# Attention and routed experts on one core: the last eight pairs of attention slots taken slot by slot

## The chip, the cores and the metric

One Trainium2 chip, one of its cores. The metric is the device time of one launch in microseconds; three runs of the kernel before gave a median of 679.24 us (677.79 to 680.12).

## The reference

```python
# q, k, v: (8, 8, 576, 64), s: (8, 8, 576); w_gate (512, 8), w_local (512, 1), w1 (8, 512, 1024), w2 (8, 1024, 512)
scores = scale * q @ k.T                              # per batch and head
cum = cumsum(maximum(s, 0))
bias = -(cum[:, None] - cum[None, :])                 # a weight of each key, falling with distance
scores = where(causal, -1e9, scores + minimum(bias, 0))
x = (exp(scores - max) / sum) @ v                     # to (batch, token, 8 heads * 64 = 512)
for b in range(8):
    for t in range(576):
        fresh = argmax(x[b, t] @ w_gate)
        e = fresh if t == 0 or sigmoid(x[b, t] @ w_local) < 0.5 else previous e
        out[b, t] = softmax(x[b, t] @ w_gate)[e] * (maximum(x[b, t] @ w1[e], 0) @ w2[e])
```

All in float32. A token's expert depends on the token before it, so the routing is a scan along each batch.

## The kernel before

The order of every instruction is written by hand: the code's order is each engine's order, and waits come from the data, from buffers that have to come free, and from events on which a transfer or a scatter is hung by `held`.

*The attention* (the first 203 us) runs over 32 slots `n`, one for a batch and two of its heads. Keys are cut in blocks of 128 and the triangle of the causal mask is skipped. A slot has

- `scores(n, u)`, u = 0, 1, 2: products of keys and queries into two PSUM banks (tile `ps`), exponential on ScalarE into tile `e`, masks of the diagonal on GpSimd (`masked`);
- `scores_halves`: the same for the 64x64 blocks that stand half over the diagonal (`ph`, `eh`, lines 1236 and 1238). `HALVES` names four of them per slot, which lie on the upper and the lower 64 partitions; a fifth, the last block (index `NH - 1`), lies on 64 partitions as well;
- `values_halves(n)` and `values(n, part)`: products of those weights with the values `vg` (lines 1288 and 1275), summed in a room of two PSUM banks, one bank for each part of the slot. Before the change the last block's products are the last steps of `values`, as 128-row products whose other 64 rows meet zeros;
- `evacuate(n, part)`: VectorE reads the sums, a reciprocal and a product for each part, into the token rows `xb`;
- `turn(n)`: a 32x32 transpose for the router; `weigh(n)`: values times key weights for a later slot (`WEIGHED` says up to which slot, after which pair).

Products in float32 take two passes, so each appears in the profile as two rows of PE and two weight loads (PEld).

Slots go in pairs `m`: scores of both slots, then the sums of both. The first slot's room is `po0`, `po1`, two banks of their own (`ps_o`); the second slot's is `pb`, taken from the ring of three two-bank buffers (`ps_s`) that also serves `ps`, `ph`, `lp` and `pos`.

*The router* works on groups of two batches, eight slots. `plan(m, place, f)` puts a piece of it into pair m: 0 and 1 behind the scores of the first and the second slot, 3 and 4 behind their sums, 5 at the pair's end. `product` (`lp`, TensorE), `logits`, `codes`, `turn1`, `turn2` (a scan on VectorE), `ranks` (`pos`, TensorE), `rows` and `gates` make each token's row in a table in DRAM; `scatter` stores 128 such rows by an indirect DMA from GpSimd, 18 times per group (`STORES` has the places). `assign_early` counts the first blocks of the experts at place 1 of pair 11.

*The loads* of later q, k and v go through SP's queue in the order of `transfers`, each hung on an exponential or a reciprocal. *The experts* (from 203 us on) work through units of tokens with weights that stream from DRAM.

The heart of the old loop over pairs:

```python
po = room(a)
values_halves(a, po, m)
halves = banks("ph") if b + 1 < NPAIR else None
to = room(b)
scores_halves(m + 1, halves)
values_halves(b, to, True)
```

## Time and profile before

| | us |
|---|---|
| median of three runs | 679.24 |
| the profiled execution | 680.58 |
| its span | 678.8 |
| attention, up to the first product of the experts | 202.57 |
| TensorE busy in the span | 662.1 |
| VectorE, GpSimd, ScalarE busy | 492.5, 369.6, 195.3 |

The profile is of one execution. "PE" are TensorE's products, "PEld" its weight loads; "issue" is idle time with no releaser in the profile. In the chain of waits a row has its start, its length, its engine, tile and line. DMA queue q8 carries instructions.

### The profile page before, as it was taken

How to read it: one execution, taken by the hardware profiler on the slowest of the kernel's cores; microseconds unless marked ns; L12 is line 12 of the kernel's file. 1: busy time of each engine (PE TensorE's matmuls, PEld its weight loads, DVE VectorE, ACT ScalarE, POOL GpSimd, SP SyncE). 2: the span in 40 equal slices, each digit the busy share in tenths (PEclk: the TensorE clock that was granted, in tenths of full speed). 3: DMA queues.
4: the chain of work that ended last, by engine and by line, in shares of the span. 5: the costliest groups of instructions: out<-in, count | busy, mean ns of one | idle time of the engine just before them, and what ended most of it. 6: DMA issues, size and time to landing. Idle time of an engine off the chain costs nothing.

```text
span 678.8 us, 18449 instructions
## 1 busy us (share of the span) xinstructions
PE 662.1 (98%) x7501; PEld 571.4 (84%) x7501; DVE 492.5 (73%) x942; ACT 195.3 (29%) x353; POOL 369.6 (54%) x525
## 2 busy tenths in 40 slices
PE   8999999999999999999999999999999999999995
PEld 7888877877788899999999999999589687796884
DVE  4665856886867799878988988955467664766843
ACT  4555635535522212212122122212211111111111
POOL 3562476776744888964555557540642542714733
PEclk9999999999999999999999999999999999999998
DMA  8665665766659798579977565616949796943002
GB/s 263 193 183 158 197 219 151 215 214 210 197 133 392 240 327 288 191 255 364 344 274 231 204 187 186 241 55 235 354 66 386 271 361 132 295 148 112 28 14 76
DMA packets 56549, 145.75 MB, mean 215 GB/s; under 512 B 13104, under 2 KB 33968, under 8 KB 51464
## 3 DMA queue, kind: packets, MB, share of 16 engines
q1 hardware_dynamic: 47352, 124.23, 55.8%
q0 software_dynamic: 9008, 20.11, 8.2%
q8 instruction: 61, 1.00, 0.6%
q14 instruction: 32, 0.26, 0.1%
q10 hardware_dynamic: 96, 0.15, 0.1%
HBM read 123.83 MB, written 20.85 MB: 213 GB/s over the span
## 4 chain that ended last, share of the span: by engine, by line
PE 86%; DVE 6%; issue 4%; POOL 2%; ACT 0%; POOLq 0%; DVEq 0%
PE p L731 26%; PE p L738 25%; PE ps L1218 11%; PE po L1275 6%; PE pb L1275 6%; PE hp L865 3%; PE yp L888 2%; PE hp L856 2%; PE lp L238 1%; PE ph L1236 1%; POOL out_dram L840 1%; DVE wt L655 1%; PE po L1288 1%; DVE w2b L655 1%; PE warm L1142 1%
## 5 line engine op out<-in xcount | busy, mean ns | idle before, releaser
L738 PE MATMUL p<-w2b,hT 128*128 128x256 f32 (+1 forms) x720 | 163.0, 379 | 0.0
L738 PEld LDWEIGHTS p<-w2b,hT 128*128 128x128 f32 (+1 forms) x720 | 133.3, 187 | 21.9 <-PE hp L856 1.6
L731 PE MATMUL p<-xTs,w1b 128*128 128x128 f32 (+1 forms) x1040 | 142.9, 295 | 0.0
L731 PEld LDWEIGHTS p<-xTs,w1b 128*128 128x128 f32 x1040 | 137.9, 191 | 3.6 <-issue 1.6
L1219 ACT ACTIVATE e<-ps 128x768 f32<-128x768 f32 (+1 forms) x96 | 76.4, 885 | 64.1 <-PE ps L1218 58.1
L840 POOL DMA_INDIRECT out_dram<-y,gi x37 | 46.9, 1269 | 74.2 <-ACT y L767 66.3
L767 ACT ACTIVATE y<-y,gi 128x256 f32<-128x256 f32 (+1 forms) x71 | 34.5, 505 | 161.6 <-DVE y L763 161.6
L771 ACT ACTIVATE hT<-hT 128x512 f32<-128x512 f32 (+1 forms) x52 | 36.8, 711 | 143.7 <-DVE hT L763 143.7
L1218 PE MATMUL ps<-qb,kb 64*128 64x384 f32 (+4 forms) x516 | 77.5, 446 | 0.2 <-ACT e L1219 0.2
L1218 PEld LDWEIGHTS ps<-qb,kb 64*128 64x128 f32 x516 | 47.7, 189 | 27.5 <-ACT e L1219 10.3
L371 POOL DMA_INDIRECT table<-xb,idx x54 | 57.3, 1062 | 15.8 <-issue 14.4
L738 PE MATMUL p<-wt,hSs 128*128 128x256 f32 (+1 forms) x272 | 63.3, 379 | 0.0
L710 POOL TENSOR_TENSOR hT<-hT,hSs 128x512 f32<-128x512 f32 (+1 forms) x14 | 21.1, 1508 | 76.8 <-PE p L738 76.8
L731 PE MATMUL p<-xSs,wt 128*128 128x128 f32 (+1 forms) x416 | 58.9, 295 | 0.5 <-DVE wt L655 0.5
L738 PEld LDWEIGHTS p<-wt,hSs 128*128 128x128 f32 (+1 forms) x272 | 50.7, 186 | 8.0
L1202 POOL TENSOR_SCALAR_AFFINE_SELECT e<-e 128x128 f32<-128x128 f32 (+1 forms) x96 | 35.7, 394 | 38.5 <-ACT e L1219 38.2
L731 PEld LDWEIGHTS p<-xSs,wt 128*128 128x128 f32 x416 | 55.6, 192 | 1.2 <-PE p L731 0.7
L763 DVE TENSOR_TENSOR hT<-p,sa 128x512 f32<-128x512 f32 (+1 forms) x48 | 31.2, 666 | 32.7 <-PE p L731 32.7
L1275 PE MATMUL pb<-vg,e 128*64 128x66 f32 x1280 | 41.9, 223 | 4.7 <-issue 4.7
L1275 PEld LDWEIGHTS pb<-vg,e 128*64 128x64 f32 x1280 | 39.7, 138 | 5.6 <-issue 5.4
L1275 PE MATMUL po<-vg,e 128*64 128x66 f32 x1280 | 41.6, 223 | 1.6 <-issue 1.6
L1275 PEld LDWEIGHTS po<-vg,e 128*64 128x64 f32 x1280 | 39.0, 138 | 3.2 <-issue 2.1
(304 smaller groups left out, 951.9 us busy)
## 6 DMA issues: line engine op xcount, KB each, us to landing
w2b<-in_w_dram SPq DMA_DIRECT2D x20, 2048.0 KB, 13.5
w1b<-in_w_dram SPq DMA_DIRECT2D x19, 2048.0 KB, 10.5
va<-in_v_dram SPq DMA_DIRECT2D x32, 320.0 KB, 3.4
xq<-table SPq DMA_DIRECT2D x72, 130.0 KB, 3.7
kb<-in_k_dram SPq DMA_DIRECT2D x31, 288.0 KB, 4.2
qb<-in_q_dram SPq DMA_DIRECT2D x31, 288.0 KB, 3.3
w1b<-in_w_dram SPq DMA_DIRECT2D x4, 512.0 KB
table<-xb,idx POOLq DMA_INDIRECT x54, 5.1
```

The source lines that it names most:

```text
L371: put = self.nc.gpsimd.indirect_dma_start(out=self.halves, in_=src, element_offset=0, in_offset=None, out_offset=bass.IndirectOffsetOnAxis ...
L710: self.adder(u, layer).tensor_tensor(a12, a12, (self.xS, self.hS)[layer][u][1], op=Alu.subtract)
L731: mm(ps[:, m * h : m * h + h], lhsT=b[:, k, (c * of + m) * P : (c * of + m) * P + P], rhs=a[:, k, :], start=m == 0 and k == 0, stop=m == o ...
L738: mm(ps[:p, c * w : c * w + w], lhsT=a[:, k, c * p : c * p + p], rhs=b[:, k, :], start=c == 0 and k == 0, stop=c == parts - 1 and k == n - 1)
L763: nc.vector.tensor_tensor(to[:, c], part, s[:, c], op=Alu.add)
L767: ins = nc.scalar.mul(to[:, c], to[:, c], gi[:p, parts * r + c, 1:2]).ins
L771: return gated(to, r) if layer else nc.scalar.activation(to, to, Act.Relu).ins
L840: put = nc.gpsimd.indirect_dma_start(out=out, out_offset=bass.IndirectOffsetOnAxis(ap=idx, axis=0), in_=y, element_offset=0, bounds_check= ...
L1202: nc.gpsimd.affine_select(out=ap, in_=ap, compare_op=Alu.is_ge, fill=0.0, base=base, pattern=n, channel_multiplier=-1)
L1218: mm(ps[:, h, at : at + z - a], lhsT=kb[d, key : key + P], rhs=qb[d, a:z], start=True, stop=True)
L1219: exps[n, u] = nc.scalar.activation(e[:, :, : WIDTH[u]], ps, Act.Exp, scale=scale).ins
L1275: of = mm(po[part][d, j - a, :], lhsT=weights_of(n, c, j, h), rhs=vgs[n % NV][:, c if j < 2 * G1 else G1 + c, h, :], start=(first and i == ...
```

## The change

- Pairs 8 to 15 are taken in halves. For n above 16: scores of slot n, the halves' scores of slot n + 1, then opening the room, halves and sums of slot n - 1, its reads and `after(n - 1)`. The values of a pair so stand behind the scores of the next slots. Slots of these pairs all use `po0`, `po1`, except the last one. The first eight pairs keep the old order.
- The last block's products move from `values` into `values_halves`, always on the lower 64 partitions. `eh` is per slot; its exponential is two instructions per slot (64 x 4 columns on 128 partitions, 128 columns on 64) and its masks are two (64x256 and 64x384).
- In pairs 8 and later `ranks`, `rows` and `gates` stand behind the first slot's sums (place 3) and not behind the second slot's scores.
- `codes` moves to a new place 2, behind the first slot's turn; the end of `turn2` becomes `turn3`, two places later; `weigh` is spread over slots; scatters are held by the end of the value products and no longer by a copy of the reciprocal; `STORES` changes.

TensorE, from slot 27's scores on before (pair 13), and from slot 26's on now (`ps` scores, `ph` halves' scores, line 1288 or 1298 the halves' products, line 1275 or 1285 the other products of values):

```order
L1218 MATMUL ps<-qb,kb 128x512 x2
L1218 MATMUL ps<-qb,kb 128x384 x2
L1218 MATMUL ps<-qb,kb 128x256 x2
L1218 MATMUL ps<-qb,kb 128x128 x2
L1288 MATMUL po_3302<-vg_137,eh 64x66 x2
L1288 MATMUL po_3303<-vg_137,eh 64x66 x2
L1288 MATMUL po_3302<-vg_137,eh 64x66 x2
L1288 MATMUL po_3303<-vg_137,eh 64x66 x2
L1236 MATMUL ph<-qb,kb 64x64 x20
L1288 MATMUL pb<-vg_138,eh 64x66 x8
L1275 MATMUL po_3302<-vg_137,e_3240 64x66 x6
```
```order
L1219 MATMUL ps<-qb,kb 128x512 x2
L1219 MATMUL ps<-qb,kb 128x384 x2
L1219 MATMUL ps<-qb,kb 128x256 x2
L1219 MATMUL ps<-qb,kb 128x128 x2
L1240 MATMUL ph<-qb,kb 64x64 x10
L1298 MATMUL po_3281<-vg_136,eh 64x66 x2
L1298 MATMUL po_3282<-vg_136,eh 64x66 x2
L1298 MATMUL po_3281<-vg_136,eh 64x66 x2
L1298 MATMUL po_3282<-vg_136,eh 64x66 x4
L1285 MATMUL po_3281<-vg_136,e_3073 64x66 x6
L1285 MATMUL po_3281<-vg_136,e_3074 64x66 x2
L1285 MATMUL po_3282<-vg_136,e_3073 64x66 x2
```

Between the scores stand the products of one slot instead of two, ph is split into ten and ten, and the last block's products (x4) stand with the halves.

VectorE, from slot 21's reads to the start of the early counting (`recs`, `xb` are the reads of the sums, `vg` a weighing, `xt` a turn, `cnt` the counting's first row):

```order
L1298 RECIPROCAL recs<-pb 128x8
L1298 TENSOR_TENSOR xb<-pb,recs 128x8x32
L1298 RECIPROCAL recs<-pb 128x10
L1298 TENSOR_TENSOR xb<-pb,recs 128x10x32
L1195 TENSOR_TENSOR vg_137<-va,wk 128x4x64
L1195 TENSOR_TENSOR vg_137<-va,wk 128x10x64
L1195 TENSOR_TENSOR vg_138<-va,wk 128x4x64
L1195 TENSOR_TENSOR vg_138<-va,wk 128x10x64
L1312 STREAM_TRANSPOSE xt_2719<-xb 128x9x2x32 x2
L388 TENSOR_TENSOR cnt<-base,base_631 128x8
```
```order
L1307 RECIPROCAL recs<-po_2755 128x8
L1307 TENSOR_TENSOR xb<-po_2755,recs 128x8x32
L1307 RECIPROCAL recs<-po_2756 128x10
L1307 TENSOR_TENSOR xb<-po_2756,recs 128x10x32
L1321 STREAM_TRANSPOSE xt_2713<-xb 128x9x2x32
L1196 TENSOR_TENSOR vg_138<-va,wk 128x4x64
L1196 TENSOR_TENSOR vg_138<-va,wk 128x10x64
L1196 TENSOR_TENSOR vg_135<-va,wk 128x4x64
L1196 TENSOR_TENSOR vg_135<-va,wk 128x10x64
L389 TENSOR_TENSOR cnt<-base,base_644 128x8
```

The two turns of a pair became one turn of a slot. Fourteen more rows of counting follow in both, and then the reads of slot 22: before, they free the room of slot 24, now that of slot 23.

GpSimd, masks and scatters (`e`, `eh` masks; `gap` and `table` one scatter) from the masks of slots 24 and 25 on before, and from those of slot 24 on now:

```order
L1202 AFFINE_SELECT e_2971<-e_2971 128x2x64
L1202 AFFINE_SELECT e_2972<-e_2972 128x2x64
L1202 AFFINE_SELECT e_2973<-e_2973 64x4x64
L1202 AFFINE_SELECT e_2995<-e_2995 128x2x64
L1202 AFFINE_SELECT e_2996<-e_2996 128x2x64
L1202 AFFINE_SELECT e_2997<-e_2997 64x4x64
L1202 AFFINE_SELECT eh<-eh 64x640
L1202 AFFINE_SELECT eh<-eh 128x640
L370 COPY gap<-recs 1x1
L371 DMA table<-xb,idx 75264x260
```
```order
L1203 AFFINE_SELECT e_2960<-e_2960 128x2x64
L1203 AFFINE_SELECT e_2961<-e_2961 128x2x64
L1203 AFFINE_SELECT e_2962<-e_2962 64x4x64
L1203 AFFINE_SELECT eh<-eh 64x256
L1203 AFFINE_SELECT eh<-eh 64x384
L371 MEMSET gap 1x1
L372 DMA table<-xb_1267,idx 75264x260
```

Six masks for a pair and two for its halves become three and two for a slot; three scatters follow each slot's masks there.

The diff, cut:

```diff
-NH = 2 * len(HALVES) + 1
+NH = len(HALVES) + 1
-WEIGHED = (3, 5, 9, 11, 11, 13, ...)
+WEIGHED = (1, 2, *(n + 2 - (n in (13, 21, 29)) for n in range(2, NPAIR)))
-STORES = (((3, 4, 5, 5, 5), ...
+STORES = (((3, 4, 5, 5, 5), (3, 4, 5, 5, 5), (3, 5, 5, 5), (3, 5, 5, 5)), ((5, 5, 5), (3, 3, 3, 5, 5, 5), (3, 3, 3, 5, 5, 5), (3, 3, 3)), ((5, 5, 5), (3, 3)))
+HALF_FROM = 8
...
         v.transpose(et, self.ei)
+        v.tensor_scalar(st["s1"], st["s1"], et[:, 31:32], None, Alu.max)
+
+    def turn3(self, g):
...
-    p_eh = pool("p_eh", 2)
+    p_eh = pool("p_eh", 3)
...
+        for j, n in enumerate(ns):
+            own = heads[1]
+            e = eh[n] = p_eh.tile([P, NH, 2, DH], F32, name="eh")
+            ps = ph[:, :, j * NH * DH : (j + 1) * NH * DH].rearrange("p h (n i) -> p n h i", i=DH)
+            for i, side, x in [*((t, side, x) for t, blocks in enumerate(HALVES) for side, x in zip(heads, blocks)), (NH - 1, own, NJ - 1)]:
...
+            nc.scalar.activation(e[:, : NH - 1], ps[:, : NH - 1], Act.Exp, scale=scale)
+            nc.scalar.activation(e[own, NH - 1], ps[own, NH - 1], Act.Exp, scale=scale)
+            for side in heads:
+                k = NH if side == own else NH - 1
+                masked(e[side, :k].rearrange("p n h i -> p (n h) i"), [[0, 2 * k], [1, DH]])
...
+    def apart_of(n):
+        return n % 2 and (n < 2 * HALF_FROM or n == NPAIR - 1)
     def room(n):
-        if n % 2:
+        if apart_of(n):
             po = banks("pb")
...
-        steps = [(j, c) for j in range(a, z) for c in [*range((j + 1) // 2), *([NF] if j == NJ - 1 else [])]]
+        steps = [(j, c) for j in range(a, z) for c in range((j + 1) // 2)]
...
     def values_halves(n, po, first):
+        todo.append((NH - 1, 1, side, NJ - 1, G1 + NF))
...
-        plan(m, 5, lambda g=g: (router.codes(g), router.turn1(g)))
+        plan(m, 2, lambda g=g: router.codes(g))
+        plan(m, 5, lambda g=g: router.turn1(g))
-        plan(m + 1, 1, lambda g=g: router.turn2(g))
+        plan(m + 1, 2, lambda g=g: router.turn2(g))
+        plan(m + 1, 5, lambda g=g: router.turn3(g))
+        p = 1 if m + 2 < HALF_FROM else 3
+        plan(m + 2, p, lambda g=g: router.ranks(g, banks))
...
-            after = {3: (2 * i, NJA), 4: (2 * i + 1, 0)}.get(p)
-            plan(i, p, lambda g=g, c=c, after=after, pair=pair: router.scatter(g, c, after, summed.get(pair)))
+            pair = {3: (2 * i, 1), 4: (2 * i + 1, 0), 5: (2 * i + 1, 1)}[p] if first else None
+            plan(i, p, lambda g=g, c=c, pair=pair: router.scatter(g, c, summed.get(pair)))
...
+        elif m < HALF_FROM:
+            of = {("e0", c): v_part(n), ("e2", c): v_part(n + 1), ("e1", c + 1): k0, ("v0", c): q0, ("v1", c): k1, ("v0", c + 1): q1}
+        else:
+            k = ("v0", c - 1) if m > HALF_FROM else ("e0", c + 1)
+            of = {("e0", c): v_part(n), ("e2", c): v_part(n + 1), k: k0, ("e1", c + 1): q0, ("e2", c + 1): k1, ("v0", c): q1} if n < NPAIR else {}
...
+    def after(n):
+        m, second = divmod(n, 2)
+        turn(n)
+        if second:
+            at(m, 5)
+        for i in range(WEIGHED[n] + 1, ...):
+            weigh(i)
+        if not second:
+            at(m, 2)
...
+        if m < HALF_FROM:
+            if second:
+                po = opened(n - 1)
+                scores_halves(n + 1, n + 2)
+                to = opened(n)
+                sums(n - 1, po)
+                sums(n, to)
+                after(n - 1)
+                after(n)
+        elif n > 2 * HALF_FROM:
+            scores_halves(n + 1)
+            sums(n - 1, opened(n - 1))
+            after(n - 1)
+    sums(NPAIR - 1, opened(NPAIR - 1))
+    after(NPAIR - 1)
```

`opened(n)` takes a room and runs `values_halves` in it; `sums(n, po)` runs `values` and `evacuate` for both parts and what is planned behind them.

## The prediction

> **What bounds the kernel now.** I read the page first, then what TensorE waits for, then the chain of waits in the attention (the first 203 us), then busy time by stretch and the DMA queues.

> ```profile
> span 678.8 us, 18449 instructions
> PE 662.1 (98%) x7501; PEld 571.4 (84%) x7501; DVE 492.5 (73%) x942; ACT 195.3 (29%) x353; POOL 369.6 (54%) x525
> ```

> TensorE is busy for 662.1 of 678.8 us, so the time is TensorE's work plus the moments in which it stands. The waits of PE in the attention are almost only these:

> ```profile
> PE pb L1275 <- issue: 4.7, 5, 1.4
> PE po L1275 <- issue: 1.6, 3, 1.1
> ```

> "issue" means that no semaphore explains the wait: eight pauses, 6.3 us, all inside the runs of value products. The chain shows where one sits (start, length, work):

> ```profile
> 41.67 4.67 PE ps L1218 x32
> 52.60 4.67 PE ps L1218 x32
> 155.99 2.31 PE lp L238 x64
> ```
> ```profile
> 165.90 4.67 PE ps L1218 x32
> 170.57 0.39 PE po L1288 x16
> 170.96 0.58 PE ph L1236 x40
> 171.54 0.23 PE pb L1288 x16
> 171.78 2.60 PE po L1275 x84
> 174.38 1.10 PE pb L1275 x37
> 175.48 1.40 issue
> 176.88 1.62 PE pb L1275 x47
> 178.50 4.67 PE ps L1218 x32
> ```

> An undisturbed pair of slots takes 52.60 - 41.67 = 10.93 us: 4.67 of scores (32 rows) and 6.26 of a burst (16+40+16+84+84 = 240 rows). The pair at 165.90 takes 12.60, which is 1.67 more for a named pause of 1.40. What the pauses are is seen when TensorE's rows are counted from the end of one to the end of the next (columns: stretch, us, PE, PEld, DVE, ACT, POOL, clock, DMA share, GB/s):

> ```profile
> 98.74:114.86 16.12, 15.03 (x383) 12.52 (x383) 9.21 (x19) 7.82 (x17) 10.63 (x19) 1.00 0.58 176
> 114.86:136.97 22.11, 21.80 (x508) 17.66 (x508) 19.20 (x58) 11.42 (x19) 14.80 (x32) 1.00 0.62 190
> 136.97:148.88 11.91, 10.62 (x254) 8.59 (x254) 10.73 (x32) 5.76 (x10) 9.30 (x19) 1.00 0.68 213
> 148.88:161.07 12.19, 11.12 (x254) 8.75 (x254) 8.13 (x16) 7.15 (x17) 8.78 (x15) 1.00 0.77 251
> 161.07:176.88 15.81, 14.41 (x383) 12.37 (x382) 12.08 (x41) 6.62 (x12) 9.38 (x19) 1.00 0.63 191
> 176.88:199.09 22.21, 21.86 (x510) 17.64 (x510) 17.30 (x48) 10.31 (x14) 15.01 (x32) 1.00 0.65 184
> ```

> PE plus PEld are 766, 1016, 508, 508, 765 and 1020 rows: with a few semaphore instructions, 3, 4, 2, 2, 3 and 4 times 256. Every pause ends at the same place in a grid of 256 instructions. The DMA queues have a partner for this. The first row is the page's; the others are the same queue in the windows 162.1 to 163.2, 118.0 to 119.1 and 174.3 to 175.5:

> ```profile
> q8 instruction: 61, 1.00, 0.6%
> q8 instruction: 1, 0.02, 5.5%
> q8 instruction: 1, 0.02, 5.4%
> q8 instruction: 1, 0.02, 5.4%
> ```

> 1.00 MB in 61 packets is 16 KB each, 64 bytes for each of 256 instructions. The third window's packet took 5.4% x 16 x 1.2 = 1.04 us, so it landed by 175.5, and TensorE resumed at 176.88, 1.4 us later. So TensorE runs out of instructions. The packet after the pause that ends at 161.07 lands by 163.2, usable (1.4 later) at 164.6: 3.5 us after the block before it was begun. After the pause that ends at 114.86 it is 119.1 + 1.4 = 120.5: 5.6 us. The same reckoning for the 22 blocks from 84 us on gives these two as the ends and 4.3 as the mean. A burst runs 480 instructions (each row has its weight load) in 6.26 us, so 256 in 3.3 us: faster than they come. The burst is starved; scores (64 instructions in 4.67 us) are not.

> [...]

> **The change, part by part.** The six stretches above hold 5.5 us of idle PE (us minus PE busy: 1.09, 0.31, 1.29, 1.07, 1.40, 0.35). With some 0.27 us per pause that the pairs lose beside it (1.67 against 1.40), seven pauses make 7.4 us in the last eight pairs.

> *Half-pair rhythm (slots 16 to 31).* One slot is now 16 score rows, 20 ph, 20 halves, 80 values: 136 rows, 272 instructions in 10.93/2 = 5.47 us. 256 in a row leave out 16 of them, 0.2 us in the burst or 1.2 in the scores, so a block lasts 4.3 to 5.2 us. Counted along the changed order from the starving place, 13 of the 16 blocks there last about 5.2 us or more, against a fetch of 4.3: they hide, but for the slowest (5.6), some 0.3 us in all. Three stay short: 3.5 and 3.6 behind the lp products (2.31 us for 64 rows) and 4.0 at the end; at 4.3 they lose 0.8, 0.7 and 0.4. Left 2.2 us (0 to 6); gain 7.4 - 2.2 = 5.2.

> *One room for all slots.* Odd slots from 17 to 29 now use the two po banks as well, so TensorE may open a slot only when VectorE has read the slot before, 2.34 + 0.29 = 2.63 us after its products. VectorE is in order; its rows around the counting of the early blocks (planned for place 1 of pair 11, before and now) are:

> ```profile
> 132.07 0.31 DVE L332 TENSOR_TENSOR at<-pos,base 128x144 f32<-128x144 f32 x1 [1.12 <-PE pos L324]
> 136.39 0.20 DVE L1298 RECIPROCAL recs<-po 128x8 f32<-128x8 f32 x1
> 138.87 0.22 DVE L1298 RECIPROCAL recs<-pb 128x10 f32<-128x10 f32 x1 [0.60 <-PE pb L1275]
> 139.54 2.22 DVE L1195 TENSOR_TENSOR vg<-va,wk 128x256 f32<-128x256 f32 x4
> 141.67 1.43 DVE L1312 STREAM_TRANSPOSE xt<-xb 128x576 f32<-128x576 f32 x2
> 143.03 0.13 DVE L388 TENSOR_TENSOR cnt<-base,base 128x8 int32<-128x8 f32 x1
> 147.75 0.20 DVE L1298 RECIPROCAL recs<-po 128x8 f32<-128x8 f32 x1
> 148.57 0.49 DVE L1298 TENSOR_TENSOR xb<-po,recs 128x320 f32<-128x320 f32 x1
> ```

> Behind slot 21's products stand in the new order: its last read (138.87 to 139.54, 0.67), one transpose (half of 143.03 - 141.67, 0.68), two weighings (141.67 - 139.54, 2.13), the counting (147.75 - 143.03, 4.72), and then slot 22's reads (149.06 - 147.75, 1.31): done at 9.5 us. TensorE wants the room at 5.47 + 2.63 = 8.1. A new wait of 1.4 us (0 if the counting shrinks to 3.2, since a dozen of its ops are short and some long; at most 1.6). Behind TensorE's wait stand only its own later products. I take +1.4.

> *Ranks behind values, turn2 in two, codes and weighings spread.* Ranks, rows and gates take 136.39 - 132.07 = 4.32 us. Behind slot 20 they make 0.67 + 4.32 + 0.68 = 5.7 in a slot of 5.47 with no weighing in it, and the next room is due 2.63 later: 0. Other pieces are smaller: 0 (to 1).

> *GpSimd: masks and scatters.* Rows of the attention, by shape:

> ```profile
> L371 POOL DMA_INDIRECT table<-xb,idx x23 | 24.5, 1065 | 6.5 <-issue 6.3 <-PE pb L1275 0.2
> L1202 POOL TENSOR_SCALAR_AFFINE_SELECT e<-e 128x128 f32<-128x128 f32 x64 | 22.7, 371 | 33.5 <-ACT e L1219 33.3
> L1202 POOL TENSOR_SCALAR_AFFINE_SELECT e<-e 64x256 f32<-64x256 f32 x32 | 14.1, 441 | 5.0 <-ACT e L1219 4.9
> L1202 POOL TENSOR_SCALAR_AFFINE_SELECT eh<-eh 64x640 f32<-64x640 f32 x16 | 12.8, 798 | 13.8 <-ACT eh L1238 13.6
> ```

> The halves' masks become two per slot, 64x256 (0.44) and 64x384 (between 0.44 and 0.80, say 0.56): 2.0 a pair, where two of 0.80 were. Three scatters (1.07 + 0.28 each, 4.0), three masks (1.18) and 1.0 make 6.2 us in a slot of 5.47, in six slots in a row: 4.4 late. A mask is wanted 8.1 us after the products that release the scatters and ready after 5.2, 2.9 spare, and the lp product adds 2.31: 0 (to 1). That scatters are now held by the products and not by the reciprocal moves them by 0.2 us: 0.

> *Last block in 64x64.* As many rows as before; a value row is 2.60/84 = 31 ns, a halves row (0.39 + 0.23)/32 = 19. 128 rows change: between -1.5 us and, where one row group alone works them off and each slot now has its own change of shape, +0.9. I take 0. ScalarE gets two small exponentials per slot for one of 640 per pair; it is busy for about half: 0.

> *Transfers.* The same loads hang on the same kinds of event, each two or more slots (11 us) ahead of use on SP's queue: 0. *First eight pairs:* same burst, grid shifted by some 20 instructions: 0.4 for a shorter block near 94 us (3.5 for 3.7).

> Sum: -5.2 + 1.4 + 0.4 = -3.4 us. Nothing behind 203 us is touched, and TensorE is busy there, so the shift reaches the end. The profiled execution took 680.58 (span 678.8, 1.8 around it), 1.3 above the median of 679.24: 680.6 - 3.4 = 677.2 there, 675.9 as a median.

> **The rivals.**
> A: the fetch doesn't fit the slot either. Loads of 288 and 320 KB now start at the same point in every slot, just ahead of the boundary, and the fetch waits among them. If it takes 5.46 on average, 13 slots lose 0.26 each, the remaining gain is gone: 679.2. For it: blocks of 5.6 are there at a DMA share of 0.6. Against: the mean is 4.3, and the stretch with the highest DMA share, 0.77 (148.88 to 161.07), ends in a pause of no more than 1.07. [...]
> B: VectorE becomes the bound of the slots, through the single room. It decides from 3.4/16 = 0.21 us of lateness per slot; at 0.5 it is 8 us more, 683.9. For it: 19.20 us of VectorE work in 22.11. Against: 2.63 us of slack which the average work (19.20/22.11 of 5.47, so 4.7 a slot) does not use up.
> C: the short blocks are fetched in the quiet 3.5 us and the counting fits: -7.0 + 0.4, 672.6.

> **How the numbers follow.** Forecast 0.58 (675.9, its own range 673.8 to 678.2), A 0.18, B 0.12, C 0.12. About 0.3% (2 us) is what can be told from no change. Faster: C, four fifths of the forecast and a little of A, 0.62; slower: B and a tail of A, 0.14; the rest 0.24. The range leaves out B and the end of C: 672.4 to 680.4.

> **What the changed profile would show.** Pauses by "issue" in slots 16 to 31 down from seven to about three, of which two lie behind lp products; slots of 5.4 to 5.5 us in the chain; one wait of PE po for VectorE of 1 to 1.6 us near slot 23; no wait for GpSimd's masks. I am wrong if pauses stand in most slots (A), if po waits for the reads in many slots (B), or if the time is given back behind the attention.

## The result: 2.8% slower, and the profile after

The changed kernel takes 698.90 us (median of four runs, 697.88 to 699.95), the kernel before 679.43 (four runs, 677.79 to 680.12): a ratio of 1.0282 (95% interval 1.0264 to 1.0301). The forecast was 675.9. The profiled execution has a span of 696.2 us instead of 678.8, and the attention ends at 219.83 us instead of 202.57: 17.3 of the 17.4 us lie ahead of the experts. One run of the changed kernel further down (c2) took 795.4 us in a slow state, at a granted clock of 0.85, and is left out there.

The page's first rows after:

```profile
span 696.2 us, 18584 instructions
PE 667.4 (96%) x7501; PEld 574.8 (83%) x7501; DVE 487.5 (70%) x941; ACT 206.8 (30%) x401; POOL 374.9 (54%) x553
```

TensorE has as many products (7501) and stands 28.8 us instead of 16.7. Busy time by stretch (columns as in the prediction) splits the attention at the first scores of slot 16. The first two rows are of the kernel before, the next two of the changed one:

```profile
9.80:100.70 90.90, 89.89 (x2269) 74.42 (x2269) 58.91 (x151) 46.99 (x84) 46.83 (x117) 1.00 0.64 199
100.70:202.57 101.87, 96.36 (x2340) 79.06 (x2337) 77.90 (x214) 49.09 (x88) 67.54 (x134) 1.00 0.62 188
```
```profile
9.80:114.64 104.84, 92.46 (x2269) 75.94 (x2269) 58.85 (x152) 53.62 (x111) 49.08 (x133) 1.00 0.56 169
114.64:219.83 105.19, 99.25 (x2341) 80.96 (x2337) 73.11 (x213) 54.06 (x109) 71.49 (x151) 1.00 0.61 186
```

The first eight pairs, whose order was to stay, lost 104.84 - 90.90 = 13.9 us; PE's idle time there went from 1.0 to 12.4 us, and its busy time for the same 2269 rows from 89.9 to 92.5. The second eight, in the new order, lost 3.3. What PE waited for in the attention after:

```profile
PE ph L1240 <- ACT eh L1242: 10.7, 9, 2.6
PE po L1285 <- POOL e L1203: 3.5, 4, 1.9
PE po L1285 <- issue: 2.3, 2, 1.4
PE pos L327 <- DVE incl L319: 1.4, 1, 1.4
```

The third row answers to the 6.3 us of "issue" before: the pauses that the change aims at are down, to what was forecast. The other three rows are new. The timeline of the changed kernel shows the first one at work, in the pair at 46.8 us (in brackets the idle time ahead and its releaser):

```profile
52.21 0.53 PE L1240 MATMUL ph<-qb,kb 64*64 64x64 f32 x17
52.99 0.41 ACT L1241 ACTIVATE eh<-ph 128x256 f32<-128x256 f32 x1
53.43 0.27 ACT L1242 ACTIVATE eh<-ph 64x128 f32<-64x128 f32 x1
53.76 0.46 PE L1240 MATMUL ph<-qb,kb 64*64 64x64 f32 x16 [1.02 <-ACT eh L1242]
```

`scores_halves(n + 1, n + 2)` issues ten products (20 rows) for one slot, then that slot's two exponentials, then ten products for the next slot into the same PSUM tile `ph`. The second ten wait until both exponentials have read the tile. It happens once in each pair, nine times ahead of slot 16.

The second new wait, on GpSimd and TensorE near slot 26:

```profile
187.50 0.54 POOL L1203 TENSOR_SCALAR_AFFINE_SELECT eh<-eh 64x384 f32<-64x384 f32 x1 [1.61 <-DMA table<-xb,idx]
188.33 0.98 POOL L372 DMA_INDIRECT table<-xb,idx  x1 [0.16 <-POOL gap L371]
189.62 1.38 POOL L372 DMA_INDIRECT table<-xb,idx  x1 [0.21 <-issue]
191.30 0.96 POOL L372 DMA_INDIRECT table<-xb,idx  x1 [0.22 <-issue]
192.31 0.90 POOL L1203 TENSOR_SCALAR_AFFINE_SELECT e<-e 128x128 f32<-128x128 f32 x3
192.66 1.15 PE L1285 MATMUL po<-vg,e 128*64 128x66 f32 x32 [1.93 <-POOL e L1203]
```

The mask `eh 64x384` waits 1.61 us for the scatters ahead of it to land, not only to be issued; then come three more scatters, and the masks that TensorE needs are 1.93 us late. In the program's list of instructions that wait is written: this mask, on partitions 64 to 127, waits for the DMA queues of the scatters before it, while the masks that start at partition 0 do not. The traces agree: in E13, which has this mask, GpSimd waits 10.5 us for scatters in six waits ahead of `eh`, and E14, whose masks start at partition 0, has no such row.

### The profile page after: what moved, and what is told of

It is laid out like the page before. It is cut to its first block, busy times and chain, and to the rows that moved or that the text cites. A ratio compares the mean times of both kernels' runs of the same rounds, so it can differ in the third digit from the quotient of the medians.

```text
span 696.2 us, 18584 instructions
## 1 busy us (share of the span) xinstructions
PE 667.4 (96%) x7501; PEld 574.8 (83%) x7501; DVE 487.5 (70%) x941; ACT 206.8 (30%) x401; POOL 374.9 (54%) x553
## 4 chain that ended last, share of the span: by engine, by line
PE 59%; DVE 5%; issue 3%; POOL 3%; ACT 0%; POOLq 0%; DVEq 0%; ACTq 0%
PE p L732 25%; PE p L739 24%; PE hp L866 3%; PE yp L889 2%; PE hp L857 2%; POOL out_dram L841 1%; DVE wt L656 1%; PE po L1285 1%; DVE w2b L656 1%; DVE w1b L656 1%; POOL table L372 1%; PE ps L1219 0%; POOL hT L711 0%; PE lp L238 0%; PE pb L1285 0%
## 5 line engine op out<-in xcount | busy, mean ns | idle before, releaser
L1219 PE MATMUL ps<-qb,kb 64*128 64x384 f32 (+4 forms) x516 | 78.1, 445 | 0.4 <-ACT e L1220 0.4
L1219 PEld LDWEIGHTS ps<-qb,kb 64*128 64x128 f32 x516 | 47.7, 189 | 27.6 <-issue 10.8
L1285 PE MATMUL po<-vg,e 128*64 128x66 f32 x1840 | 59.7, 223 | 5.8 <-POOL e L1203 3.5
L372 POOL DMA_INDIRECT table<-xb,idx x54 | 56.3, 1042 | 14.8 <-issue 11.6
L1285 PEld LDWEIGHTS po<-vg,e 128*64 128x64 f32 x1840 | 56.0, 138 | 8.0 <-POOL e L1203 4.1
L1203 POOL TENSOR_SCALAR_AFFINE_SELECT eh<-eh 64x256 f32<-64x256 f32 x64 | 32.5, 507 | 30.3 <-ACT eh L1241 13.0
L1307 DVE RECIPROCAL recs<-po 128x8 f32<-128x8 f32 (+1 forms) x46 | 9.7, 211 | 51.2 <-PE po L1285 47.1
```

What stands on the lines that cost most here:

```text
L372: put = self.nc.gpsimd.indirect_dma_start(out=self.halves, in_=src, element_offset=0, in_offset=None, out_offset=bass.IndirectOffsetOnAxis ...
L1203: nc.gpsimd.affine_select(out=ap, in_=ap, compare_op=Alu.is_ge, fill=0.0, base=base, pattern=n, channel_multiplier=-1)
L1219: mm(ps[:, h, at : at + z - a], lhsT=kb[d, key : key + P], rhs=qb[d, a:z], start=True, stop=True)
L1285: of = mm(po[part][d, j - a, :], lhsT=weights_of(n, c, j, h), rhs=vgs[n % NV][:, c if j < 2 * G1 else G1 + c, h, :], start=(first and i == ...
```

## The experiments

The runs fell on several chips. On some the kernel before takes 680 us, as in the result, on others 685. Every ratio is to the kernel before on the same chip; it is estimated from all the runs and differs by up to 0.3% from the quotient of the two medians. The halves are the stretches of the table above, read from each trace: up to the first scores of slot 16, and from there to the first product of the experts.

| run | before there | us | ratio (95%) | halves, us |
|---|---|---|---|---|
| before, result's trace | 679.4 | | | 90.9, 101.9 |
| changed, result's trace | 679.4 | 698.9 | 1.0282 (1.0264 to 1.0301) | 104.8, 105.2 |
| changed again (c4) | 680.4 | 697.4 | 1.0263 (1.0236 to 1.0290) | 106.4, 103.5 |
| E13 | 679.5 | 686.5 | 1.0112 (1.0089 to 1.0135) | 93.9, 104.7 |
| E14 | 679.5 | 682.5 | 1.0039 (1.0014 to 1.0065) | 97.3, 98.4 |
| E10 | 680.4 | 690.9 | 1.0145 (1.0128 to 1.0162) | 96.5, 110.5 |
| E11 | 680.4 | 693.3 | 1.0184 (1.0167 to 1.0201) | 100.2, 107.7 |
| E12 | 680.4 | 689.1 | 1.0129 (1.0100 to 1.0159) | 97.1, 105.2 |
| before (c1) | 684.9 | 686.0 | | 94.9, 103.6 |
| changed (c2) | 684.9 | 713.9 | 1.0451 (1.0411 to 1.0492) | 107.9, 119.4 |
| before (c3) | 685.0 | 684.7 | | 94.4, 102.7 |
| E1 | 685.3 | 703.6 | 1.0253 (1.0195 to 1.0310) | 96.6, 118.6 |
| E2 | 685.3 | 709.7 | 1.0337 (1.0283 to 1.0391) | 108.8, 114.5 |
| E3 | 685.3 | 700.4 | 1.0209 (1.0156 to 1.0262) | 99.3, 113.2 |
| E4 | 685.3 | 702.4 | 1.0233 (1.0179 to 1.0287) | 97.3, 116.9 |
| E5 | 684.9 | 704.0 | 1.0280 (1.0259 to 1.0300) | 101.3, 111.7 |
| E6 | 684.9 | 702.1 | 1.0253 (1.0233 to 1.0272) | 97.4, 113.2 |
| E7 | 685.0 | 687.1 | 1.0026 (1.0013 to 1.0039) | 95.9, 104.4 |
| E8 (E6 again) | 685.0 | 702.6 | 1.0261 (1.0233 to 1.0288) | 100.5, 113.1 |
| E9 | 685.0 | 705.8 | 1.0293 (1.0267 to 1.0320) | 100.9, 118.8 |

### E1, E13: products of both slots ahead of the exponentials

```diff
-        for j, n in enumerate(ns):          # products, exponentials, masks of one slot, then of the next
+        for n, ps in zip(ns, pss):          # the products of both slots
+            ...
+        for n, ps in zip(ns, pss):          # then exponentials and masks of both
```

> The changed kernel, but scores_halves issues the 64x64 score products of both blocks before the exponentials and masks of either; nothing else differs. Theory T (the first half lost its time where the second block's ph products wait for the exponentials of the first block's, 14.8 us summed over nine runs of ph products, 13.9 us net in the first eight pairs): the run of 40 ph products is back at 0.54 us, the second half begins near 101 us instead of 114.64, and the time is 698.9 - 13.9 = 685.0 (684 to 686.5). Rival U (ScalarE's two small exponentials a block and GpSimd's masks are themselves too long for a pair): their number is the same here, so the wait only moves to the values of the halves, and the time stays above 695. Masks behind the scatters are unchanged: the second half stays at about 105.2 us in both.

> The changed kernel with the score products of both blocks ahead of the exponentials and masks, nothing else (as the first experiment), for a chip on which the kernel before takes 680 us. There theory T says: no ph wait, second half begins at 101 to 103 us instead of 115.9, the mask waits of 2.3 to 3.5 us and the pos wait of 1.4 us stay, pair of 550 instructions: 697.4 - 13 = 684.4 (683 to 686), ratio 1.004 to 1.008. On a chip with trickling: 1.0253 again. Rival U (much of the ph wait was spent on fetching instructions, which then stops PE elsewhere, as the runs with 566 instructions a pair show with 3 us in the first half): ratio 1.010 to 1.013.

PE's waits in E13 (the products of values now stand in line 1287):

```profile
PE po L1287 <- POOL e L1203: 3.0, 3, 2.5
PE po L1287 <- issue: 2.6, 3, 1.4
PE pos L327 <- DVE incl L319: 1.4, 1, 1.4
PE pb L1287 <- issue: 1.1, 2, 0.9
```

The row of ph is gone, in E1 as well, and the first half is 93.9 us instead of 104.8. Against the changed kernel's ratios of 1.0282 and 1.0263, E13 takes back 1.5 to 1.7%, 10 to 12 us: the largest part of the loss. E13 is 2.1 us slower than theory T's 684.4, and the ratio falls where rival U put it. What is left of the first half's loss is 3.0 us, of which 1.4 are the pos wait and 1.0 come of undisturbed pairs of 11.05 instead of 10.93 us (8 x 0.12). The 1.1 us of instruction pauses in the pb rows stand in the first half, where the kernel before has 0.9 and the changed kernel none; that much of rival U is there. On its chip E1 gave 703.6, far from the 685 expected; that led to the next question.

### E2, E3: masks that start at partition 0

```diff
-            for i, side, x in [..., (NH - 1, own, NJ - 1)]:
+            for i, side, x in [..., (NH - 1, own, NJ - 1), (NH - 1, heads[0], NJ - 1)]:
-            nc.scalar.activation(e[:, : NH - 1], ...); nc.scalar.activation(e[own, NH - 1], ...)
-            for side in heads: masked(e[side, :k] ...)
+            nc.scalar.activation(e, ps, Act.Exp, scale=scale)
+            masked(by[:DH], [[0, 2 * NH], [1, DH]]); masked(by, [[0, 2 * NH], [1, DH]], DH)
```

> The changed kernel, but the last block's product is made on both halves of the partitions (two more 64x64 products a block, the extra result unused), so that one exponential does for a block and the masks start at partition 0 as before the change; the instruction order of the masks then holds no wait on the scatters' DMAs. Theory T (3.5 us of PE's idle time in slots 180.64 to 202.39 come from a mask that waits for the scatters to land): no wait of po on a mask above 0.3 us there, second half 105.2 - 3.5 = 101.7 us; the first half keeps its ph wait, shorter by the second exponential (about 0.2 us in nine places, 1 to 3 us in all): time 693.5 (692 to 695). Rival U (the masks are late because GpSimd is busy issuing the scatters, about 1 us each): the waits stay, the second half stays above 104.5, and the time is above 696.

> The changed kernel with both edits: products of both blocks ahead of the exponentials, one exponential a block and masks from partition 0. Theory T: the two losses are independent and add up: 698.9 - 13.9 - 3.5 = 681.5 (680 to 683), with slots of 5.70 us in the second half and 2 to 3 us of PE pauses without a releaser. So still not faster than before (679.4), since a slot of the second half is 0.23 us longer than half a pair (16 x 0.23 = 3.7 us) and this eats most of what the shorter pauses give (7.4 - 2.3 = 5.1 us). Rival U (waits of the first half were hiding pauses of the instruction stream, which come back): first half longer than 103 us, time 685 or more.

E2 to E3 on one chip is the ph wait alone: 9.3 us. Neither came near its figure, which had been reckoned for a chip with 680 us. No wait for a mask above 0.3 us is left in them, but E2 stands 8.3 and E3 11.3 us in pauses by "issue".

### c1, c2: the same chip with its own traces

> The kernel before itself, for a trace from the same chip as the runs beside it. Theory F (the chip of the first four experiments gave the kernel before 685.3 us and not 679.4 because PE's instructions come later there, as the pauses without a releaser in those traces do: 12 us in the first of them, where the changed kernel had 2.3 us on its chip): if this chip is like that one, the time is 683 to 687 and the pauses sum to 10 to 14 us where the other chip's trace of before had 6.3 us; else 678 to 681 and 6 to 7.5 us. Rival G (the extra 6 us lie behind the attention): the attention ends at 202 to 204 us as before.

> The changed kernel itself, for a trace and a ratio from the same chip. Theory T: ratio 1.025 to 1.03, the first half about 13 us longer than that of the kernel before, with ph runs of 2.0 us and more, and 3 to 4 us of waits of po on masks. If the instruction pauses are longer on this chip, they come to more than 2.3 us in the second half here too. Rival G: the ratio depends on the chip and the ph wait is shorter here.

Theory F was wrong in size: the kernel before pauses 6.7 us in c1, not 10 to 14. Of the 5.7 us by which c1's two halves are longer than those of the result's trace, 3.9 stand as busy time of TensorE (190.2 instead of 186.2 us) and not as pauses; what makes products longer there is not known. In c2 the ph wait of the changed kernel is as long as before (11.0 us), but the ratio is 1.0451 and not 1.025 to 1.03, and there the pauses differ. The timeline of c2, PE's values and GpSimd's scatters:

```profile
149.29 0.98 POOL L372 DMA_INDIRECT table<-w2b,idx  x1 [0.16 <-POOL gap L371]
149.84 0.51 PE L1285 MATMUL po<-vg,e 128*64 128x66 f32 x9
150.57 1.19 POOL L372 DMA_INDIRECT table<-w2b,idx  x1 [0.21 <-issue]
150.59 0.35 PE L1285 MATMUL po<-vg,e 128*64 128x66 f32 x3 [0.24 <-issue]
151.31 0.35 PE L1285 MATMUL po<-vg,e 128*64 128x66 f32 x4 [0.38 <-issue]
152.02 0.36 PE L1285 MATMUL po<-vg,e 128*64 128x66 f32 x5 [0.36 <-issue]
152.06 0.96 POOL L372 DMA_INDIRECT table<-w2b,idx  x1 [0.23 <-issue]
152.75 0.37 PE L1285 MATMUL po<-vg,e 128*64 128x66 f32 x5 [0.37 <-issue]
153.48 0.70 PE L1285 MATMUL po<-vg,e 128*64 128x66 f32 x17 [0.36 <-issue]
```

While a burst of scatters is in flight, about five rows of products come every 0.73 us where some 23 do otherwise (84 in 2.60 us); the expectations call this trickling. On the chips with 685 us the changed order has many short pauses (by "issue" in the po rows 21 of up to 0.4 us in c2, 7.6 us in all, and 20 of up to 1.1 us in E1, 8.5 us) and the kernel before fewer (in c1 eight in the pb row, 3.8 us); on the chips with 680 us the changed kernel has two, of 2.3 us together, in the result's trace and one of 0.3 us in c4. So what goes with a scatter differs by chip, and in the changed order more of a burst meets short products: a burst of three takes 3.7 us in c2 (149.29 to 153.02), the scores above it now 2.4 instead of 4.67.

### E4, E5, E6: pair order and half order with the rest equal

```diff
-HALF_FROM = 8
+HALF_FROM = 16                                  # E4, E5, on top of E3
-        p = 1 if m + 2 < HALF_FROM else 3
+        p = 3                                   # E5, E6
```

> The kernel of both edits with the half-pair order taken out: HALF_FROM 16, all sixteen pairs in the old pair order; what is left of the change is the last block's 64x64 products, the places of the scatters and of the rank steps. Theory T (the 0.23 us a slot come from changing between 128-row and 64-row products once a block instead of once a pair): a pair without other work is back at 10.93 us (10.85 to 11.0), the pauses of the second half are back at 6 to 7.5 us, and the time is 679.4 (678.5 to 681). Rival U (the 0.23 us come from the last block's products, which are now among the 64-row ones): a pair is 11.3 to 11.4 us and the time 684 to 687.

> The run in the old pair order (last block's 64x64 products, products first, one exponential, masks from partition 0) with the rank steps of all groups behind the first block's values instead of ahead of the pair. Theory T: the three waits of the pos products on VectorE (1.4, 2.2 and 1.9 us, 5.6 together, and 2.9 us of ps behind VectorE's evacuations) were made by the later rank steps meeting the old place, and vanish: 7 to 9 us less than the run without this edit, ratio to before 1.010 to 1.014. Rival U (VectorE as a whole is too late): the wait of 5.6 us moves to other products and the ratio stays at 1.02 or above.

> The run with both edits (products first; one exponential and masks from partition 0), in the half-pair order of the change, with the one rank step that stood ahead of a pair (first group) behind values too. Theory T: the one wait of 1.4 us and the 0.6 us behind it vanish: ratio 1.018, that is 2 us less than 1.0209. Against the run in the old pair order on this chip it tells what the half-pair order is worth when all else is equal: theory T says slots longer by 16 x 0.23 = 3.7 us against pauses shorter by 5 us, so the half-pair order is 1 to 2 us faster; rival V (pauses without a releaser don't shorten on a chip where instructions come late): half-pair order 3 to 6 us slower.

E4 was expected at the time of the kernel before and is 2.3% slower: with the old order of pairs and both waits gone, the rest of the change still costs. Its pos products wait 5.6 us, three times, since the later `turn3` meets the old place of `ranks`. An undisturbed pair takes 11.05 us, between theory T's figure and rival U's. In E5 the waits of pos are gone as expected, but 2.7 us of ps behind VectorE's reads stay, and no time came of it (on another chip than E4, so not closely comparable). Neither E5 nor E6 reached its ratio (1.010 to 1.014, and 1.018). E6 against E5 is the half order alone: 1.9 us faster, within what theory T had, but the two intervals overlap, so this is not clear of noise.

### E7: one more change of shape in the kernel before

```diff
-        values_halves(b, to, True)      # ahead of the first slot's values
         ...
+        values_halves(b, to, True)      # behind them
```

> The kernel before, with one move: the second block's 64-row products of values and diagonal weights stand behind the first block's 128-row values instead of ahead of them. Same products, but 128-row and 64-row products change twice a pair more. Theory T (each round trip from 128-row to 64-row products and back costs 0.4 to 0.5 us, which is the 0.23 us a slot of the changed order): pairs of 10.93 become 11.35 to 11.45 us, time 6.5 to 8 us longer, ratio 1.009 to 1.012. Rival U (the 0.23 us are the price of waiting for ScalarE's exponentials of ph or of the products' own number): pairs stay at 10.9 to 11.0 and the ratio is 1.000 to 1.003.

The chain of waits in E7, one pair:

```profile
31.58 4.67 PE ps L1218 x32
36.25 0.39 PE po L1288 x16
36.64 0.58 PE ph L1236 x40
37.23 2.60 PE po L1275 x84
39.83 0.39 PE pb L1288 x16
40.22 2.60 PE pb L1275 x84
42.82 4.67 PE ps L1218 x32
```

A pair is 42.82 - 31.58 = 11.24 us instead of 10.93: the same products with one more round trip from 128-row to 64-row products and back cost 0.31 us, less than theory T's 0.4 to 0.5. Sixteen make 5 us, but the median rose by 2.1 only, so the ratio falls in rival U's range though the pair does not. In c3, the trace of the kernel before from the same chip, two pairs are undisturbed at 10.93 us, and the same two take 11.24 in E7. The others, in which pauses and scatters fall, came out between 1.0 us shorter and 1.0 us longer. Why was not found: pauses by "issue" are 3.6 us in c3 and 3.2 in E7.

### E8, E9, c3: scatters let go earlier, two at a time

```diff
-STORES = (..., ((5, 5, 5), (3, 3, 3, 5, 5, 5), ...
+STORES = (..., ((5, 5), (3, 3, 5, 5), (3, 3, 5, 5), (3, 3, 5, 5), (3, 3, 3, 3)), ((5, 5), (3, 3, 5)))
-            pair = {3: (2 * i, 1), ..., 5: (2 * i + 1, 1)}[p]
+            pair = {3: (2 * i, 0), ..., 5: (2 * i + 1, 0)}[p]      # from pair 8 on
```

> The changed order with both edits and the rank steps behind values again, as the control on this chip for the run beside it. On a chip with trickling: 1.0253 as before, 10 us of pauses within scatter bursts. On a chip without: theory T says slots of 5.70 us, 2 to 3 us of pauses on the grid, no masks waiting for scatters, and 680 to 681.5 us, a ratio of 1.000 to 1.004; rival U (the first half or the slots are longer for another cause) a ratio above 1.01 there too.

> The same kernel, with the scatters of the second half two at a time instead of three and let go by the end of the first part of the values instead of the second, so that a burst lies under the next block's 128-row score products (2.2 us, few instructions) rather than under values (some 50 instructions a us). Theory S: pauses within bursts fall from 10 us to 3 to 5 us and the time by 5 to 7 us against the run beside it (ratio about 1.016 on a chip with trickling; no difference on one without). Rival W (the pauses come with the number of scatters, wherever they stand): 9 to 11 us stay and the time is within 2 us.

Inconclusive: E9 is 3.2 us slower than E8, which neither theory had. Pauses by "issue" fell from 12.6 us in E8 to 8.3 in E9, but new waits took their place, of ph for VectorE's index arithmetic (4.8 us once, where I had put four scatters behind the rank steps) and of ph for exponentials (4.0). The kernel before took 684.7 us in c3, as in c1, with 3.6 us of pauses by "issue" instead of 6.7.

### E10, E11, E12, c4: the router's steps and the scatters back

```diff
+        plan(m, 5, lambda g=g: (router.codes(g), router.turn1(g)))
+        plan(m + 1, 1, lambda g=g: (router.turn2(g), router.turn3(g)))
+        p = 1                                   # all three; E10 and E11 in pair order, E12 in half order
+            after = {3: (2 * i, NJA), ...}      # E11: STORES and the scatters' events of the kernel before
```

> Pair order, products first, one exponential and masks from partition 0 (ratio 1.0233 with the rank steps in the change's places, 1.028 with all of them behind values), with the router's turns and rank steps back in the places they had before the change. Theory P (splitting and delaying the router's steps makes VectorE hand over the scatters' indices 2 us later against the pair, so the first burst of scatters of a group leaves the score products and runs into 64-row products and values): waits of pos on VectorE gone, excess within bursts back from 10 to 12 us to 5 to 7 us, ratio 1.012 to 1.017. Rival Q (what lets each scatter go, PE's last product instead of VectorE's reciprocals, is what shifts them): within 0.3% of 1.0233, bursts still above 9 us.

> The run beside it with the table of scatter places and what lets each go as before the change too. What is left of the change: the last block's 64x64 products among the 64-row ones (two more 64x64 products a block than the change has), weights of the diagonal in a tile per block, order of turns and of value weights on VectorE. Theory P: pairs of 11.04 instead of 10.93 us (0.11 x 15 = 1.7 us) and otherwise like before: ratio 1.001 to 1.006. Rival L (the last block's part itself costs what remains, in bursts or in pairs): ratio above 1.012.

> The half-pair order of the change in the second eight pairs, products first, one exponential, masks from partition 0 (ratio 1.0209 to 1.0261 in three runs), with the router's steps back in their old places. Theory P: 3 to 5 us less in bursts and no wait of 1.4 us of pos: ratio 1.014 to 1.019; still slower than before, since slots of 5.70 us cost 3.7 us and triples of scatters outlast the 2.2 us of score products of one block. Rival Q: within 0.3% of 1.0253.

> The changed kernel itself on the chip of the runs beside it, for the sum: ratio 1.045 on a chip where the kernel before takes 685 us, 1.028 where it takes 679.4. The steps from it to the run with scatters back are to add up to what the change cost there.

This chip has no trickling, so these ratios read against the result. E10's ratio lies in theory P's range and E12's just below it (1.0129 against 1.014 to 1.019), but P is about pauses within bursts, which this chip does not have, so they do not bear it out. E11 (1.0184 against 1.001 to 1.006) is far from it, so P fails as an account of the whole. E11 is the kernel before but for the last block's products, a tile of weights per slot and the order of turns and weighings, and costs 13 us. Its waits:

```profile
PE po L1290 <- issue: 5.7, 4, 2.4
PE ps L1223 <- DVE xb L1312: 3.7, 3, 1.7
PE pb L1290 <- issue: 1.9, 5, 0.7
```

With the two added products E11 has 560 instructions a pair (280 rows of PE, each with its load) instead of 544, so a grid of 256 instructions falls elsewhere in each pair, and pauses come in the first half too: 4.9 us there, where the kernel before has 0.9, and 9.8 in all against 6.3. The waits for VectorE come on top, and one stretch at half clock (see the end); the 13 us were not added up in full. E12 against E10 is the half order alone, here 1.8 us faster; the intervals overlap again, and E10 has a wait of 2.4 us for a load of q that E12 has not. But E12's second half has a new row, the one that the prediction feared from the single room:

```profile
PE po L1299 <- DVE recs L1308: 3.6, 2, 2.0
```

### E14: half order, both waits gone, ranks behind values

E14 is E6's kernel on a chip without trickling.

> Half-pair order, products first, one exponential, masks from partition 0, rank steps behind values and the turns in the change's places, for a chip on which the kernel before takes 680 us. Against the run with the router's steps back (ratio 1.0129, 4.1 us of waits of values on VectorE's reciprocals in the second half and 1.3 us in the first): theory R (those waits come from the rank steps standing ahead of the evacuations on VectorE, which the change's split avoids) says they vanish: 5 us less, 684 us, ratio 1.004 to 1.008, with the second half at 101 us (16 slots of 5.70, no pauses). On a chip with trickling: 1.025 as before. Rival Q: they stay and the ratio is 1.011 or above on a chip with 680 us.

```profile
9.55:106.85 97.30, 92.56 (x2341) 76.33 (x2341) 58.03 (x152) 49.30 (x93) 51.46 (x134) 1.00 0.60 182
106.85:205.26 98.41, 98.36 (x2396) 80.61 (x2393) 72.90 (x213) 50.35 (x95) 69.60 (x150) 1.00 0.65 199
```
```profile
117.24 2.36 PE ps L1219 x16
119.60 0.51 PE ph L1240 x24
120.10 0.35 PE po L1299 x20
120.46 2.48 PE po L1286 x80
122.94 2.36 PE ps L1219 x16
```

In the second half PE stands 0.05 us in 98.41: no pause, no mask, no VectorE. A slot is 122.94 - 117.24 = 5.70 us. The half is 3.5 us faster than in the result's trace of the kernel before. As theory R said, the waits for VectorE's reciprocals are gone. The whole kernel is still 0.4% slower, for its first half takes 97.3 us instead of 90.9: pauses of 1.5 us and less, which end 252 and 508 rows of PE apart (at 21.90, 32.52 and 53.62 us; with their loads about 2 and 4 times 256 instructions, on a grid shifted against the pairs of 280 rows), pairs of 11.05 us, and one wait of 1.5 us for masks.

No run beat the kernel before. E13's first half, without its pos wait (93.9 - 1.4), and E14's second (98.4) would make 190.9 us where the kernel before has 192.8: an estimate of 1.9 us, about what can be told from no change; it was not run, and how the instruction grid would fall in it is not known.

## Why the prediction was wrong

*The step that failed* is "First eight pairs: same burst, grid shifted by some 20 instructions: 0.4", with "ScalarE gets two small exponentials per slot [...]; it is busy for about half: 0". The first eight pairs keep their order of calls, but the function that they call became a loop over slots, with exponentials between products that share a PSUM tile. I costed ScalarE by its load, and did not ask who waits for the new exponential. The first half cost 13.9 us instead of 0.4. E13, whose edit moves these products and nothing else, shows 10 to 12 of them to be that wait (11.0 in the halves of the two traces).

*The pauses of instructions*, -5.2, was right: 2.3 us by "issue" are left in the second half, in two pauses that both lie behind lp products, against 2.2 forecast. That the sizes agree so closely is luck, for the same kernel has 0.3 us in c4, and E14 none: there nothing was lost behind the short blocks either, as rival C had it. Rival A, that the fetch wouldn't fit the slot either, is out.

*Last block in 64x64: 0, between -1.5 and +0.9* was mis-sized: slots of 5.70 us instead of 5.47 are 16 x 0.23 = 3.7 us, outside my bounds. E13 splits them in one trace. Its pairs in the old order take 11.05 instead of 10.93 us, so 0.06 a slot come with the last block's part and not with the half order; its slots in the half order take 5.70, so the half order adds the other 0.17, or 0.35 in two slots. What I named and rounded away, each slot's own change of shape, has that size: E7's round trip costs 0.31 us. It is not quite the same change, for E7 goes from values to halves and back, and the half order goes once more through scores, halves and values. The 3.7 us ate most of the gain. E7's 0.31 us a pair agree with a cost at each change of shape; what TensorE does in that time, no run here shows.

*GpSimd: 0 (to 1)* was 3.5 us in the result's trace. My spare 2.9 us counted the issue of three scatters; one mask waits for their landing, as the program's list of instructions shows. Masks from partition 0 have no such wait, and E14's second half no wait for a mask. Why the mask on partitions 64 to 127 is given that wait is not settled.

*One room: +1.4 near slot 23* did not come: among PE's waits in the result's trace is none of po for VectorE. The mechanism is real, though: E12, with the rank steps ahead of the reads, has 3.6 us of it. *Ranks behind values, turn2 in two: 0 (to 1)* hid its opposite in the first half, where the later `turn3` meets the old place of `ranks`: one wait of 1.4 us, and three of 5.6 together in E4.

In sum: first half +13.9; second half -5.1 (pauses) + 3.7 (slots) + 3.5 (masks) = +2.1 of the +3.3 measured; the other 1.2 us were not separated. An estimate: the forecast's 0.27 us lost beside each pause, for the two pauses and four mask waits that are left, would make 1.6.

## What to carry to other kernels

When a helper changes from one block per call to a loop over blocks, cost it at every place that calls it, and look for a reader between two writers of one PSUM tile: issue all products first. A bound that names the mechanism (a change of shape per slot) must be priced from a row of that transition, for 0.2 us sixteen times is the size of the gain. And where instructions limit TensorE, count them per loop turn: 16 more in a pair left an undisturbed pair at 11.05 us (E13 without them, E14 with them) but moved the 256-instruction grid, and pauses in the first half were 2.9 (E14) and 4.9 us (E11) instead of 1.1 (E13).

## What the runs showed of the hardware that I had not expected

```profile
70.00:71.00 1.00, 1.00 (x48) 0.93 (x42) 0.00 (x0) 0.65 (x2) 0.59 (x2) 1.00 0.00 0
71.00:72.00 1.00, 1.00 (x28) 1.00 (x24) 0.63 (x2) 0.23 (x2) 0.72 (x2) 0.53 0.06 16
72.00:73.00 1.00, 1.00 (x24) 1.00 (x22) 0.00 (x0) 0.00 (x0) 0.00 (x0) 0.50 0.50 115
73.00:74.00 1.00, 1.00 (x24) 1.00 (x22) 0.00 (x0) 0.00 (x0) 0.00 (x0) 0.50 0.48 180
74.00:75.00 1.00, 1.00 (x32) 1.00 (x30) 0.26 (x2) 0.22 (x1) 0.00 (x0) 0.77 0.00 0
75.00:76.00 1.00, 1.00 (x42) 1.00 (x38) 0.97 (x3) 0.00 (x0) 0.00 (x0) 1.00 0.14 18
```

  The four rows with a clock under 1.00 lack 1.7 us in all; at the 0.50 of the two rows in the middle that makes 3.4 us, an estimate. In those two rows 24 rows of products come in a us, in the rows around 48 and 42; the pair took 1.6 us more than in the result's trace, on top of the wait's 2.6. The clock fell to 0.50 after waits of 1.9 to 2.6 us also in c2 (70 to 72 us), again in c4 (194 to 197), in E10 (143 to 145), E11 (95 to 97) and E12 (187 to 189). It stayed at 1.00 after the same wait of 2.6 us in the result's trace, after one of 2.5 in E13 and after one of 2.2 in E11 (208 to 210). What decides between the two, no run here shows.
- On two chips TensorE paused often while scatters were in flight, in the changed order above all (7.6 us in 21 pauses in c2, 8.5 us in 20 in E1); in c2's timeline about five rows of products come every 0.73 us. The kernel before took 685 us there instead of 680, and the changed one, on one of them, 714 instead of 698. That the scatters cause it was not shown (E9 was inconclusive), and what differs between the chips is not known.
